# Gate computation moved to the next step, and head work moved between engines, in a fused retention and mixture-of-attention-heads kernel

## The chip, the cores and the metric

The kernel runs on one core of one Trainium2 chip. The metric is the device time of one execution, in microseconds (µs); the median of three executions is 523.59 µs (520.85 to 524.5).

The core has five engines that run side by side, each through its own list of instructions in order: TensorE (PE; its weight loads are shown as PEld), VectorE (DVE), ScalarE (ACT), GpSimd (POOL) and SyncE (SP, which issues the DMAs here). An instruction that has to wait holds up all that stand behind it on its engine.

## The reference

Two layers, in float32. The first is retention over 8 batches, 8 heads, 576 tokens and head size 64: `ret = 0.125 * (q k^T) * D`, with `D[i,j] = gamma_h^(i-j)` for `j <= i` and 0 above, and `x = ret v`. Heads side by side give `x` of shape (8, 576, 512). The second layer is a soft mixture of four causal attention heads ("experts") over `x`:

```
logits = x @ w_gate                      # (B, S, 4); the two largest are kept per token
w = softmax of the two kept              # divided by (sum + 1e-9)
q, k, v = x @ wq[e], x @ wk[e], x @ wv[e]
a = softmax(causal(0.125 * q k^T))       # divided by (sum + 1e-9)
out += mask_e * w_e * (a @ v @ wo[e])    # over the four experts
```

## The kernel before, in words

**Tiling.** Tokens of a batch are cut into chunks of 128, 128, 128, 128 and 64 (`CH`), which makes 40 chunks over the 8 batches. For the second layer they form two ranges: chunks 0 and 1 (256 tokens) and chunks 2 to 4 (320 tokens), `RNG`. Products that need more precision than one pass are made from a high and a low part (`xh`, `xl`, `wh`, `wl`): three passes of float32r matmuls.

**The loop.** The main loop (L494) runs steps n = 0 to 41, then `end()` follows. Step n computes the retention scores of chunk n (`qk`), finishes chunk n-1 (`result`: matmuls `old` and `own`, the product with the decay table `gi`, and the split into `xh` and `xl`), updates the running state from chunk n (`state`: matmuls `st`, sums `s`), starts the attention of tile n-6 (`scores`: matmuls `ss`, then softmax on DVE and ACT), transposes the probabilities of tile n-7 (`turn`: matmuls `pt` and copies to `pth`), does a share of projection work (`work`), normalizes tile n-6 (`normal`, DVE) and multiplies tile n-7 with the values (`values`: matmuls `ys`).

**Projection work.** `STEPS` sets it for each batch b: q and k of the first range in step 5b+3 and of the second in 5b+6 (`proj`, matmuls `pj`), values and gate logits of the first range in 5b+5 and of the second in 5b+7 (`vproj`, matmuls `pv`, results `vn` and `lg`), output projections in 5b+9 and 5b+12 (`outproj`, matmuls `po`). Batch 0 does its first parts piece by piece in steps 2 to 5, and the last batch some a step earlier.

**The gate.** `gate` (L260 to L284) makes the weights `wt` from the logits: ten small DVE groups (L268 to L284) with one exponential on ACT between them (L278), for which DVE waits. It is called by the last `vproj` of a range (L257). `normal` (L339) multiplies `wt` of its own tile's range into the reciprocal sums and scales the probabilities `p32` (L355). For tiles t = 0 and t = 2, the first of a range, that is one step after the `vproj` that ends the range.

**Order and buffers.** PE, DVE, ACT and POOL run in exactly the order in which the code issues to them (`manual_schedule`); the DMAs of SP are put in place by the framework. All PSUM tiles share one ring of eight banks (L49), so a matmul group also waits for the reader of the tile eight places before it.

**Head.** `decay(n+1)` (L92) in step n scales v of chunk n+1 by `gam` and, for chunks 1 to 4, makes that chunk's part of the table `gi` out of its first 128 columns; before the change both are POOL instructions, apart from chunk 0's v scaling on DVE. `result` multiplies by `gi` and makes `xl` on DVE for chunks 0 to 3 and on POOL from chunk 4 on (L182). Raw weights are fetched by `fetch` into two buffers (L198) and split by `weights` into high and low part (ACT L209, DVE L210): q and k in step 1, v in step 4, o in step 6.

## Time and profile before

| | |
|---|---|
| three executions | 523.59, 520.85, 524.5 µs |
| the profiled execution | 522.38 µs, its span 520.7 µs |
| PE busy, share of the span | 91% |
| DVE, ACT, POOL busy | 62%, 49%, 42% |
| mean TensorE clock granted, as a share of full speed | 0.961 |
| DMA traffic | 50.98 MB, mean 98 GB/s |

A row of the profile names engine, line and tiles as out<-in. In a timeline the first two numbers are the start in µs from the start of the span and the time from the first start to the last end of the instructions merged into the row (x4: four of them); a bracket at the end gives the idle time of the engine before the row and the instruction that ended it. In a table of waits the numbers are total µs, how often, and the longest. In a table of windows PEclk is the clock granted to TensorE in that stretch, 1.00 being full speed.

### The profile page before, as it was taken

The numbers are of one execution on the slowest core, as the hardware profiler recorded it, in microseconds if no ns is written. First come the engines' busy times: TensorE is split into PE (matmuls) and PEld (weight loads), VectorE is DVE, ScalarE is ACT, GpSimd is POOL, SyncE is SP. The second block draws the span as 40 slices with busy tenths as digits, with TensorE's granted clock in tenths as the row PEclk, the third lists the DMA queues.
The fourth block names the chain that finished last, engine by engine and source line by source line (L and its number), as shares of the span: only waits on it lengthen the run. The fifth ranks groups of instructions, "written<-read, shape, count | busy, mean of one in ns | idle before, by whom it ended". The sixth has DMA issues, their size and how long they took to land.

```text
span 520.7 us, 19016 instructions
## 1 busy us (share of the span) xinstructions
PE 472.8 (91%) x7996; PEld 413.5 (79%) x7996; DVE 323.4 (62%) x1136; ACT 256.8 (49%) x798; POOL 221.2 (42%) x279
## 2 busy tenths in 40 slices
PE   5768989999898989989899898989899898998996
PEld 3668968788788868889688797879788896877785
DVE  3655586754787556782767638775468737584463
ACT  2344546445464435645465354644447453654462
POOL 3834544543364434544246344554345443420201
PEclk9787989999899998999899998999989999999999
DMA  8943223404151241413223142431405101001022
GB/s 301 336 172 125 82 83 114 132 8 146 66 199 48 82 133 61 146 43 132 85 83 124 41 134 83 139 108 52 164 21 186 44 13 41 3 2 42 1 72 71
DMA packets 22516, 50.98 MB, mean 98 GB/s; under 512 B 2720, under 2 KB 11680, under 8 KB 22432
## 3 DMA queue, kind: packets, MB, share of 16 engines
q1 hardware_dynamic: 22432, 49.77, 27.8%
q8 instruction: 63, 1.03, 0.9%
q14 instruction: 21, 0.17, 0.1%
HBM read 40.33 MB, written 9.44 MB: 96 GB/s over the span
## 4 chain that ended last, share of the span: by engine, by line
PE 72%; DVE 17%; ACT 4%; issue 4%; DMA 2%; POOL 1%; SPq 0%; DVEq 0%; ACTq 0%; POOLq 0%
PE pj L224 22%; PE pv L248 11%; PE po L417 10%; PE pt L370 8%; PE ys L392 7%; PE ss L307 4%; PE ss L316 3%; PE qk L134 2%; DVE p L355 2%; DVE x L178 2%; DVE s L122 2%; DMA gi<-gi 2%; PE own L173 2%; PE st L114 1%; PE old L163 1%
## 5 line engine op out<-in xcount | busy, mean ns | idle before, releaser
L334 ACT ACTIVATE p<-p,nm 128x128 f32<-128x128 f32 (+4 forms) x144 | 83.0, 578 | 108.9 <-DVE nm L326 85.3
L355 DVE TENSOR_SCALAR p<-p,sm 128x128 f32<-128x128 f32 (+4 forms) x144 | 87.1, 663 | 1.4
L185 POOL TENSOR_TENSOR xl<-x,xh 128x512 fp32r<-128x512 f32 (+1 forms) x36 | 42.5, 1181 | 100.0 <-ACT xh L184 100.0
L370 PEld LDWEIGHTS pt<-con,p 128*128 128x128 f32 (+1 forms) x400 | 43.6, 143 | 49.1 <-issue 20.9
L370 PE MATMUL pt<-con,p 128*128 128x128 f32 (+1 forms) x400 | 58.3, 286 | 25.3 <-DVE x L178 12.9
L406 POOL CAST yh<-y 128x256 fp32r<-128x256 f32 (+1 forms) x39 | 15.9, 409 | 129.9 <-ACT y L405 129.9
L178 DVE TENSOR_TENSOR x<-x,own 128x256 f32<-128x256 f32 (+1 forms) x80 | 26.2, 360 | 65.2 <-ACT x L166 65.2
L326 DVE CUSTOM_DVE_ANT_0 p<-ss,mask 128x512 f32<-128x512 f32 (+3 forms) x128 | 56.2, 481 | 9.5 <-PE ss L307 7.9
L140 POOL TENSOR_SCALAR_AFFINE_SELECT p<-p 64x512 f32<-64x512 f32 (+1 forms) x80 | 49.6, 620 | 24.5 <-ACT p L137 21.7
L392 PE MATMUL ys<-pth,vn 128*64 128x128 f32 (+2 forms) x960 | 56.6, 262 | 0.0
L183 POOL TENSOR_TENSOR x<-x,gi 128x512 f32<-128x512 f32 (+1 forms) x36 | 41.7, 1159 | 27.9 <-DVE x L178 13.2
L392 PEld LDWEIGHTS ys<-pth,vn 128*64 128x64 f32 (+1 forms) x960 | 46.2, 136 | 8.1 <-issue 3.1
L253 DVE COPY lg<-pv 128x4 f32<-128x4 f32 (+1 forms) x40 | 6.4, 161 | 65.3 <-ACT vn L252 65.2
L307 PE MATMUL ss<-k,q 64*64 64x512 f32 (+3 forms) x512 | 43.8, 434 | 0.8 <-ACT p L137 0.5
L101 POOL TENSOR_TENSOR vk<-vk,con 128x512 f32<-128x512 f32 (+1 forms) x39 | 42.0, 1077 | 0.1
L373 DVE COPY pth<-pt 128x512 f32<-128x512 f32 (+3 forms) x80 | 37.7, 483 | 4.7 <-PE pt L370 4.3
L114 PE MATMUL st<-vk 64*64 64x64 f32 x1024 | 24.7, 224 | 10.0 <-POOL vk L101 5.5
L375 ACT ACTIVATE pth<-pt 128x512 f32<-128x512 f32 (+3 forms) x80 | 33.2, 420 | 0.5 <-PE pt L370 0.4
L248 PE MATMUL pv<-whv,xh 128*128 128x260 f32 (+1 forms) x160 | 27.1, 292 | 4.0 <-ACT whv L209 4.0
L224 PE MATMUL pj<-xh,whk 128*128 128x320 f32 (+1 forms) x128 | 27.9, 348 | 2.1 <-DVE s L122 1.3
L137 ACT ACTIVATE p<-qk 128x256 f32<-128x256 f32 (+1 forms) x80 | 24.6, 360 | 10.7 <-PE qk L134 10.6
L114 PEld LDWEIGHTS st<-vk 64*64 64x64 f32 x1024 | 20.4, 137 | 11.6 <-POOL vk L101 5.9
(89 smaller groups left out, 1034.2 us busy)
## 6 DMA issues: line engine op xcount, KB each, us to landing
x<-xf SPq DMA_DIRECT2D x32, 512.0 KB, 4.1
vk<-vkf SPq DMA_DIRECT2D x32, 512.0 KB, 5.4
out<-ot SPq DMA_DIRECT2D x32, 160.0 KB, 1.9
out<-ot SPq DMA_DIRECT2D x32, 128.0 KB, 1.8
raw<-wraw SPq DMA_DIRECT2D x4, 512.0 KB, 7.6
x<-xt SPq DMA_DIRECT2D x8, 256.0 KB, 2.8
vk<-vkt SPq DMA_DIRECT2D x8, 256.0 KB, 2.9
gi<-gi SPq DMA_DIRECT2D x1, 256.0 KB, 7.9
```

The costliest lines, as they stand in the source:

```text
L114: mm(ps[r][HALF[g], s, u], vk[HALF[r], s, 1, h], vk[HALF[r], s, 0, h], start=True, stop=True)
L140: gp.affine_select(w, w, pattern=[[0, 4 * k], [1, 64]], base=0, channel_multiplier=-1, compare_op=OP.is_ge, fill=0.0)
L185: e.tensor_sub(xl[:, :, l0:l0 + C], x32, f(xh[:, :, l0:l0 + C]))
L224: mm(ps, ww[:, kc, p * 128:(p + 1) * 128], xx[:, kc], start=(i == 0), stop=(i == 11))
L248: mm(ps[:C], xx[:, kc, l0:l0 + C], ww[:, kc], start=(i == 0), stop=(i == 11))
L307: mm(ps[2 * p + z][HALF[i]], q[p][HALF[z], l0 + 64 * i:l0 + 64 * i + 64], k[p][HALF[z], :w], start=True, stop=True)
L326: v.tensor_tensor_reduce(p32[:, e], ps[e], mask[:, 512 - w:], -1.0, BIG, OP.add, OP.min, nm[:, e:e + 1])
L334: act(p32[:, e], p32[:, e], AF.Exp, bias=bias, scale=-1.0, accum_out=sm[:, 0, e:e + 1])
L355: v.tensor_scalar(p32[:, e], p32[:, e], rs[:, e:e + 1], None, op0=OP.mult)
L370: nc.tensor.transpose(pt[rows, j - j0], p32[:, e, c0:c0 + jw], ident)
L392: mm(py[64 * z:64 * z + 64, p], VN[b, rr][0][jr, j - 2 * rr, e * D:(e + 1) * D], src, start=(j == 0), stop=(j == t))
L417: mm(ps, ww[:, p, d * 128:(d + 1) * 128], yy[:, p], start=(i == 0), stop=(i == 5))
```

## The change

1. `vproj` no longer calls `gate`; it notes the range in the list `GATES`. The new `gates()` computes what is noted there. The loop calls it in the next step, behind the softmax and the transposes' copies and ahead of `weights`, `work` and `normal`; `end()` calls it behind `values(LAST + 1)`.
2. In `decay` the parts of `gi` are made by four ACT instructions each (one for each of four column groups, with `fac` as scale) in place of one POOL instruction. The v scaling of chunks 1 to 3 moves from POOL to DVE.
3. In `result` the product with `gi` and the split of chunks 2 and 3 move from DVE to POOL.
4. `raw` has three buffers; the third weights (v) are fetched in step 1 and split in step 3, in place of steps 2 and 4.

```diff
@@ decay
         if 0 < n < 5:
-            gp.tensor_mul(gi[:, :, t0:t0 + C], gi[:, :, :C], fac[:, c].unsqueeze(2).to_broadcast([128, 4, C]))
-        (gp if n else v).tensor_mul(vv, vv, gam[...])
+            for kc in range(4):
+                act(gi[:, kc, t0:t0 + C], gi[:, kc, :C], AF.Copy, scale=fac[:, c, kc:kc + 1])
+        (gp if n > 3 else v).tensor_mul(vv, vv, gam[...])
@@ result
-        e = gp if n > 3 else v
+        e = gp if n > 1 else v
@@ fetch
-        RAW[n] = raw = ld.tile([128, kc, w], F32, name="raw", bufs=2)
+        RAW[n] = raw = ld.tile([128, kc, w], F32, name="raw", bufs=3)
@@ vproj
         if t == tiles[-1]:
-            gate(b, r)
+            GATES.append((b, r))
         yield
+    GATES = []
+    def gates():
+        while GATES:
+            gate(*GATES.pop())
@@ end
         values(LAST + 1)
+        gates()
         normal(LAST + 3)
@@ main loop
-        if n in (2, 4):
-            fetch("v" if n == 2 else "o")
+        if n in (1, 4):
+            fetch("v" if n == 1 else "o")
...
         run(turns)
-        for w in {1: "kq", 4: "v", 6: "o"}.get(n, ""):
+        gates()
+        for w in {1: "kq", 3: "v", 6: "o"}.get(n, ""):
             weights(w)
```

TensorE's list of instructions stays as it is, row for row. Three places where the other lists change follow. Line numbers of the changed file are higher by 1 in the first layer and by 8 from `gate` on.

DVE at the seam of steps 12 and 13 (batch 1's second range ends in step 12). Before, the end of the gate stands between the logits and the normalization (`sm`, `p`), which stands ahead of step 13's `x` and `s`:

```order
L277 TENSOR_TENSOR ex<-lg,mx 128x12
L279 SCALAR_TENSOR_TENSOR ex<-rk,ex 128x12
L280 TENSOR_REDUCE mx<-ex 128x3
L281 TENSOR_SCALAR mx<-mx 128x3
L282 RECIPROCAL mx<-mx 128x3
L284 TENSOR_TENSOR wt<-ex,mx 128x12
L346 TENSOR_SCALAR sm<-sm 128x4
L347 RECIPROCAL sm<-sm 128x4
L349 TENSOR_TENSOR sm<-sm,wt 128x4
L355 TENSOR_SCALAR p_2042<-p_2042,sm 128x256 x4
L178 TENSOR_TENSOR x_2225<-x_2225,own 128x2x128 x2
```

The same place in the changed kernel, from the copies of the logits on:

```order
L254 COPY lg<-pv 128x4 x2
L254 COPY lg<-pv 64x4
L256 COPY lg<-pv 64x4
L354 TENSOR_SCALAR sm<-sm 128x4
L355 RECIPROCAL sm<-sm 128x4
L357 TENSOR_TENSOR sm<-sm,wt 128x4
L363 TENSOR_SCALAR p_2054<-p_2054,sm 128x256 x4
L179 TENSOR_TENSOR x_2219<-x_2219,own 128x2x128 x2
L123 TENSOR_TENSOR s<-st,s 128x128 x4
```

Between the logits and the normalization the gate is gone; its rows (L276 to L292 there) follow behind step 13's softmax and last copy `pth`, ahead of step 13's own normalization.

ACT over step 13 in the changed kernel, from the values of step 12 (`vn`) to the first projection read out in step 13 (`k`); before the change the row `ex` stood between the two rows `vn 64x256` and `y`:

```order
L253 ACTIVATE vn_2122<-pv 128x256 x2
L253 ACTIVATE vn_2122<-pv 64x256
L413 ACTIVATE y_2184<-ys 128x256
L138 ACTIVATE p<-qk 128x256 x2
L167 ACTIVATE x_2219<-old 128x256 x2
L342 ACTIVATE p_2294,sm<-p_2294,nm 128x384 x2
L383 ACTIVATE pth<-pt 128x256
L342 ACTIVATE p_2294,sm<-p_2294,nm 128x384 x2
L383 ACTIVATE pth<-pt 128x256
L185 ACTIVATE xh_2215<-x_2219 128x4x128
L286 ACTIVATE ex<-ex 128x12
L230 ACTIVATE k_2344<-pj 128x256
```

The exponential of the gate now comes behind the step's softmax and its `xh`, and ahead of the projections' copies.

POOL in the head of the changed kernel, from step 0 to step 5; `AFFINE_SELECT` is the causal mask of `qk`:

```order
L141 AFFINE_SELECT p<-p 64x512 x8
L184 TENSOR_TENSOR x_438<-x_438,gi 128x512
L186 TENSOR_TENSOR xl_435<-x_438,xh_434 128x4x128
L102 TENSOR_TENSOR vk<-vk,con 128x256
L141 AFFINE_SELECT p<-p 64x256 x2
L184 TENSOR_TENSOR x_566<-x_566,gi 128x512
L186 TENSOR_TENSOR xl_435<-x_566,xh_434 128x4x128
L102 TENSOR_TENSOR vk<-vk,con 128x2x256
```

Before, each of the first three pairs of masks was followed by a `gi` and a `vk` row, and the rows `x` and `xl` of chunks 2 and 3 stood on DVE. The v scaling of chunk 5 (the last row) now stands behind the split of chunk 3.

## The prediction

> **What bounds the kernel now.** The page's busy times and its chain of work that ended last come first:

> ```profile
> PE 472.8 (91%) x7996; PEld 413.5 (79%) x7996; DVE 323.4 (62%) x1136; ACT 256.8 (49%) x798; POOL 221.2 (42%) x279
> PE 72%; DVE 17%; ACT 4%; issue 4%; DMA 2%; POOL 1%; SPq 0%; DVEq 0%; ACTq 0%; POOLq 0%
> ```

> TensorE carries the span, and the change leaves its list of work as it is. To be won are the 48 µs in which it is idle (520.7 less 472.8), and whatever it loses by running below full clock. DVE, with 17% of the chain, is what it mostly waits for. The table of TensorE's waits says where:

> ```profile
> PE pt L370 <- DVE x L178: 12.9, 8, 1.8
> PE pt L370 <- DVE p L355: 8.4, 7, 1.3
> PE st L114 <- ACT y L405: 1.7, 7, 0.5
> ```

> The transposes `pt` make up 21.3 of it, in 7 or 8 waits each: about one of each kind per batch. The timeline at the start of step 13, right behind the gate of step 12, shows the place of the longer kind:

> ```profile
> 127.18 0.21 DVE L268 TENSOR_TENSOR gd<-lg 128x48 f32<-128x48 f32 x1
> 128.35 0.21 ACT L278 ACTIVATE ex<-ex 128x12 f32<-128x12 f32 x1 [1.56 <-DVE ex L277]
> 129.44 1.51 PE L307 MATMUL ss<-k,q 64*64 64x384 f32 x15
> 130.06 0.16 DVE L346 TENSOR_SCALAR sm<-sm 128x4 f32<-128x4 f32 x1
> 132.30 0.74 DVE L178 TENSOR_TENSOR x<-x,own 128x256 f32<-128x256 f32 x2
> 132.77 0.77 PE L370 MATMUL pt<-con,p 128*128 128x128 f32 x4 [1.82 <-DVE x L178]
> 133.76 0.54 DVE L326 CUSTOM_DVE_ANT_0 p<-ss,mask 128x384 f32<-128x384 f32 x1
> 133.79 1.09 PE L370 MATMUL pt<-con,p 128*128 128x128 f32 x4 [0.25 <-DVE s L122]
> 137.09 0.63 PE L224 MATMUL pj<-xh,whq 128*128 128x256 f32 x4
> 138.52 0.64 PE L224 MATMUL pj<-xh,whk 128*128 128x256 f32 x4
> 141.46 1.09 PE L392 MATMUL ys<-pth,vn 128*64 128x128 f32 x16
> ```

> The gate holds DVE from 127.18 to 130.06. Only then come the normalization and the sums `x` and `s`, for whose banks the transposes wait 1.82 and 0.25 µs. Behind it lies a second loss, which the windows show:

> ```profile
> 73.00:75.00 2.00, 2.00 (x11) 2.00 (x10) 2.00 (x8) 1.99 (x7) 0.16 (x1) 0.50 0.03 8
> 134.00:136.00 2.00, 2.00 (x11) 2.00 (x11) 2.00 (x10) 1.66 (x6) 0.50 (x1) 0.50 0.04 8
> 441.00:443.00 2.00, 2.00 (x11) 2.00 (x11) 1.66 (x8) 2.00 (x8) 0.00 (x0) 0.50 0.00 0
> 137.00:141.00 4.00, 4.00 (x36) 4.00 (x35) 3.31 (x7) 1.95 (x7) 2.03 (x2) 1.00 0.00 0
> ```

> Behind the gap TensorE is full, but its granted clock is 0.50; from 137 on it is 1.00 again. The first and the last of the seven such seams are quoted; all seven have it. The gate of a first range costs less:

> ```profile
> 160.45 0.19 DVE L268 TENSOR_TENSOR gd<-lg 128x32 f32<-128x32 f32 x1
> 162.65 0.16 DVE L346 TENSOR_SCALAR sm<-sm 128x2 f32<-128x2 f32 x1
> 165.19 1.55 PE L370 MATMUL pt<-con,p 128*128 128x128 f32 x10 [1.12 <-DVE p L355]
> 167.00 0.82 PE L224 MATMUL pj<-xh,whk 128*128 128x320 f32 x4 [0.26 <-DVE s L122]
> 165.00:168.00 3.00, 2.47 (x17) 2.03 (x18) 3.00 (x19) 0.70 (x4) 1.28 (x1) 1.00 0.12 44
> ```

> There TensorE waits 1.12 and 0.26, and the clock stays at 1.00.

> **The change part by part.**

> *Gate of a second range* (seven seams). The normalization starts at 127.18 in place of 130.06. It takes 2.24 (130.06 to 132.30), so `x` runs from 129.42 to about 130.1 and `s` to 130.9; ACT no longer sits 1.56 µs idle at `ex`, so `x` has its input by then. TensorE ends `ss` at 130.95 (129.44 + 1.51), or some 0.3 earlier, as the wait of `st` for `y` (1.7 µs in 7 times, 0.24 each) goes too. So the waits of 1.82, 0.25 and 0.24 vanish: 2.31. What is late next: the first projection needs the bank that the softmax's first reduction frees, 0.54 behind `s`, at 131.4, when eight transposes from 130.6 on are done at 131.45. I charge 0.15 for it. For the clock: from 132.77 to 141.46 are 8.69, 0.25 of it wait. The price at full clock, and the cover for what follows below:

> ```profile
> 137.28 0.62 ACT L184 ACTIVATE xh<-x 128x512 fp32r<-128x512 f32 x1
> 144.19 0.75 DVE L178 TENSOR_TENSOR x<-x,own 128x256 f32<-128x256 f32 x2 [3.63 <-ACT x L166]
> 145.57 1.53 PE L370 MATMUL pt<-con,p 128*128 128x128 f32 x12
> 146.85 0.48 PE L417 MATMUL po<-yh,who 128*128 128x256 f32 x2
> 177.85 0.75 DVE L178 TENSOR_TENSOR x<-x,own 128x256 f32<-128x256 f32 x2 [4.90 <-ACT x L166]
> ```

> Twelve transposes take 1.28 from start to start (145.57 to 146.85), so eight take 0.85; twelve projections (137.09 to 138.52) take 1.43, so 48 take 5.72. The clock costs 8.69 - 0.25 - 6.57 = 1.87. The sum is 2.31 + 1.87 - 0.15 = 4.0 per seam, 28.0 for seven; the bounds are 2.16 (idle alone) and 4.18 (nothing new late).

> [...]

> *Gate of a first range* (six seams). DVE's 2.2 µs (160.45 to 162.65) go, and with them the waits of 1.12 and 0.26; the ten transposes and the second wait took 1.81 (165.19 to 167.00), and take 1.07 at the pace above. So 1.38 to 1.86 are saved. I take 1.7, nearer the upper end, because `s` is then done before `pt` ends: 10.2. The last batch's gate has a `pt` wait of this kind too (the seventh of the 8.4 µs): 1.0, with bounds 0.5 and 1.2.

> *Where the gate goes.* Its 2.9 or 2.2 µs land behind a softmax, in steps full of projections. Behind it on DVE stand that step's normalization and the next `x`, for which transposes and banks wait one step later. DVE idles 3.63 and 4.90 ahead of these `x`. The faster projections take 1.3 of the 3.63, so `x` would come 0.6 later at worst, and TensorE comes to it only 1.4 later (144.19 to 145.57). So it costs nothing; without that idle time all 2.9 would come back. On ACT the copies `k` and `q` stand behind `ex`, and their banks are needed again only eight tiles on.

> *Head.* These rows carry it:

> ```profile
> 11.24 1.04 POOL L100 TENSOR_TENSOR gi<-gi,con 128x512 f32<-128x512 f32 x1 [3.32 <-DMA gi<-gi]
> 36.18 1.24 PE L248 MATMUL pv<-whv,xh 128*128 128x260 f32 x4 [4.03 <-ACT whv L209]
> 41.21 0.69 PE L114 MATMUL st<-vk 64*64 64x64 f32 x32
> 45.92 0.69 PE L114 MATMUL st<-vk 64*64 64x64 f32 x32 [1.00 <-POOL vk L101]
> 47.11 0.94 PE L307 MATMUL ss<-k,q 64*64 64x128 f32 x16 [0.49 <-ACT p L137]
> 47.97 1.30 PE L224 MATMUL pj<-xh,whk 128*128 128x320 f32 x4
> L375 ACT ACTIVATE pth<-pt 128x128 f32<-128x128 f32 x16 | 4.0, 257 | 0.0
> L334 ACT ACTIVATE p<-p,nm 128x128 f32<-128x128 f32 x32 | 12.5, 393 | 25.9 <-DVE nm L326 25.9
> L183 POOL TENSOR_TENSOR x<-x,gi 128x512 f32<-128x512 f32 x28 | 35.9, 1281 | 24.6 <-PE pt L370 12.4 <-DVE x L178 10.5 <-POOL p L140 0.4
> L185 POOL TENSOR_TENSOR xl<-x,xh 128x512 fp32r<-128x512 f32 x28 | 36.6, 1307 | 83.7 <-ACT xh L184 83.7
> ```

> The trace has no ACT copy of 128 columns with a scale from memory; the nearest are a plain copy, 257 ns, and an exponential with a bias, 393. Four make 1.0 to 1.6; I take 1.1, by the copy. (1) The first four wait for the DMA of `gi` (11.2) ahead of ACT's copies of `x`, and the second four stand ahead of the q and k split; the v scaling on DVE gains back most of it. I put the first projections 0.5 later (0 to 1). (2) `whv` now stands ahead of chunk 3's copies, so `pv` can start near 33. But chunk 3's product and split now run on POOL (1.28 + 1.31) ahead of chunk 5's v scaling, whose `st` then starts near 39.7 in place of 41.21, behind a new gap of about 4 µs and so at half clock. Of the 4.03 I keep 0.6. (3) In step 6 the waits of 1.00 and 0.49 go with the gate's hold on ACT, 1.5; four projections took 1.30 there and 0.82 at 167.00, so with no gap ahead of them three such groups save 1.4. Sum: -0.5 + 0.6 + 1.5 + 1.4 = 3.0, bounds -1 and 6. The earlier fetch and third buffer of the v weights bring nothing by themselves: the split waited for ACT's order, not for a DMA.

> *Sum.* 28.0 + 10.2 + 1.0 + 3.0 = 42.2. The profiled execution took 522.4 (span 520.7), so 480.2. The median of the three runs is 1.2 above that execution and their lowest 1.5 below it, so I predict 480.

> **The rivals.**

> [...]

> *The gate's wait only moves.* If the normalization behind it ended after TensorE stands at the next `pt`, the 2.9 or 2.2 would come back as idle time there, the clock would fall there instead, and only the head's 3.0 would stay: 519. Against it stand the 3.63 and 4.90 µs in which DVE idles.

> *Slower: `ex` comes back late.* DVE stands in order behind ACT's `ex`, and ACT comes to it only after `xh`, which waits for POOL. Behind `ex` DVE needs 4.7 (128.35 to 132.30, and 0.74) until `x` is done, and TensorE needs it 9.8 behind the first projection (145.57 less 134.5, less 1.3). If `ex` starts later than 5 behind that projection, every further µs is idle time in 13 steps, plus 1.9 of clock; at 7.5 it would be 13 x (2.5 + 1.9) = 57 against the 42 gained: 537. Against it: `xh` is over at 137.9, 3.4 behind the first projection.

> **How the numbers follow.** Chances: the forecast 0.76, the slow clock stays 0.16, the wait moves 0.05, slower 0.03. The forecast's own best case is 522.4 - 7 x 4.18 - 6 x 1.86 - 1.2 - 6 = 475; a µs below it for the lowest of the runs makes the low end 474. The high end is the first rival's 498; the other two, 0.08, lie outside. A measurement of this kernel tells about 1% from no change. The first two cases are faster by more than that, 0.92; within 1% lies the moved wait, 0.05; slower is the last, 0.03.

> **What would show it.** Right: the waits of `pt` for `x` and `p` fall from 21.3 to under 4 µs, the windows with 0.50 behind the seams are gone and the mean clock rises from 0.961 to about 0.99; 48 projections behind a seam take 5.7; and in the head `st` of chunk 5 waits about 4 µs for POOL. Wrong: a `pt` wait for `p` one step later, windows of 0.50 that stay behind the seams, or DVE waiting at `ex` for more than 1 µs.

## The result, and the profile after

The changed kernel takes 484.34 µs (median of 4 runs, 482.29 to 485.27) against 523.34 (4 runs, 520.85 to 524.5) beside it: a ratio of 0.9255, 95% interval 0.9211 to 0.93. The forecast was 480, the range 474 to 498: faster, as forecast, by 4.3 less than forecast. The profiled execution took 484.3, its span 482.6, at a mean clock of 0.982.

The busy times and the chain that ended last, then the largest waits of TensorE (total µs, times, longest), after the change:

```profile
PE 458.3 (95%) x7996; PEld 401.6 (83%) x7996; DVE 314.0 (65%) x1135; ACT 260.0 (54%) x814; POOL 216.0 (45%) x276
PE 80%; DVE 9%; ACT 5%; issue 2%; DMA 2%; POOL 1%; SPq 0%; DVEq 0%; ACTq 0%; POOLq 0%
```

```profile
PE pt L378 <- DVE x L179: 3.5, 7, 0.6
PE old L164 <- DVE s L123: 2.9, 1, 2.9
PE st L115 <- POOL vk L102: 2.9, 1, 2.9
PE pj L225 <- ACT xh L185: 2.8, 1, 2.8
PE pt L378 <- DVE s L123: 1.7, 7, 0.2
```

DVE's share of the chain falls from 17% to 9%. The waits of `pt` for `p` are gone; those for `x` fall from 12.9 to 3.5. TensorE is idle for 24 µs (482.6 less 458.3) instead of 48, and its busy time falls by 14.5 with the same 7996 matmuls. By an estimate 9.3 of that is the slow clock behind the seven seams (1.33 each, worked out below); the rest was not split up. The windows behind two seams now show it at full clock:

```profile
182.50:184.50 2.00, 2.00 (x18) 2.00 (x18) 1.97 (x9) 2.00 (x8) 0.00 (x0) 1.00 0.06 18
238.50:240.50 2.00, 2.00 (x20) 2.00 (x19) 1.97 (x11) 2.00 (x8) 0.00 (x0) 1.00 0.19 78
```

No window behind any of the seven seams is below 1.00. One seam of the changed kernel in the timeline (the third of the seven; the one shown at 127 to 141 before was the second):

```profile
177.05 0.17 DVE L354 TENSOR_SCALAR sm<-sm 128x4 f32<-128x4 f32 x1
177.77 2.55 DVE L363 TENSOR_SCALAR p<-p,sm 128x256 f32<-128x256 f32 x4
177.80 0.73 POOL L415 TENSOR_TENSOR yl<-y,yh 128x256 fp32r<-128x256 f32 x1
178.49 1.43 POOL L141 TENSOR_SCALAR_AFFINE_SELECT p<-p 64x512 f32<-64x512 f32 x2
178.69 1.50 PE L315 MATMUL ss<-k,q 64*64 64x384 f32 x16
180.25 0.74 DVE L179 TENSOR_TENSOR x<-x,own 128x256 f32<-128x256 f32 x2
180.71 0.77 PE L378 MATMUL pt<-con,p 128*128 128x128 f32 x4 [0.52 <-DVE x L179]
181.73 0.63 PE L378 MATMUL pt<-con,p 128*128 128x128 f32 x4 [0.25 <-DVE s L123]
182.31 0.74 PE L225 MATMUL pj<-xh,whk 128*128 128x256 f32 x4
185.99 1.26 DVE L287 SCALAR_TENSOR_TENSOR ex<-rk,ex 128x12 f32<-128x12 f32 x1 [0.59 <-ACT ex L286]
188.19 1.09 PE L400 MATMUL ys<-pth,vn 128*64 128x128 f32 x16
```

The gate now runs behind the softmax, and DVE waits 0.59 for its exponential. But the normalization ahead of it takes 3.20 (177.05 to 180.25), not 2.24 as before: the scaling of `p` took 1.61 then (from 130.77) and takes 2.55 now. So TensorE still stops twice at the seam, 0.52 and 0.25, where I had charged 0.15 in all.

### The profile page after: what moved, and what is told of

Its sections match the earlier page's. It is cut to its first block, busy times and chain, and to the rows that moved or that the text cites. A ratio compares the mean times of both kernels' runs of the same rounds, so it can differ in the third digit from the quotient of the medians.

```text
span 482.6 us, 19026 instructions
## 1 busy us (share of the span) xinstructions
PE 458.3 (95%) x7996; PEld 401.6 (83%) x7996; DVE 314.0 (65%) x1135; ACT 260.0 (54%) x814; POOL 216.0 (45%) x276
## 4 chain that ended last, share of the span: by engine, by line
PE 80%; DVE 9%; ACT 5%; issue 2%; DMA 2%; POOL 1%; SPq 0%; DVEq 0%; ACTq 0%; POOLq 0%
PE pj L225 21%; PE pv L249 11%; PE ys L400 10%; PE po L425 10%; PE pt L378 9%; PE ss L315 5%; PE qk L135 4%; DVE p L363 3%; PE ss L324 3%; PE own L174 2%; PE st L115 2%; PE old L164 2%; DVE x L179 2%; DMA gi<-gi 2%; ACT p L138 1%
## 5 line engine op out<-in xcount | busy, mean ns | idle before, releaser
L186 POOL TENSOR_TENSOR xl<-x,xh 128x512 fp32r<-128x512 f32 (+1 forms) x38 | 44.6, 1174 | 97.3 <-ACT xh L185 97.3
L363 DVE TENSOR_SCALAR p<-p,sm 128x128 f32<-128x128 f32 (+4 forms) x144 | 70.7, 551 | 1.4
L414 POOL CAST yh<-y 128x256 fp32r<-128x256 f32 (+1 forms) x39 | 17.5, 449 | 112.2 <-ACT y L413 112.2
L378 PEld LDWEIGHTS pt<-con,p 128*128 128x128 f32 (+1 forms) x400 | 42.7, 139 | 28.7 <-issue 12.5
L334 DVE CUSTOM_DVE_ANT_0 p<-ss,mask 128x512 f32<-128x512 f32 (+3 forms) x128 | 56.2, 482 | 8.5 <-PE ss L315 8.5
L378 PE MATMUL pt<-con,p 128*128 128x128 f32 (+1 forms) x400 | 55.1, 280 | 7.0 <-DVE x L179 3.5
L184 POOL TENSOR_TENSOR x<-x,gi 128x512 f32<-128x512 f32 (+1 forms) x38 | 44.5, 1170 | 13.5 <-PE pt L378 8.7
L102 POOL TENSOR_TENSOR vk<-vk,con 128x512 f32<-128x512 f32 (+1 forms) x36 | 35.3, 980 | 0.0
L413 ACT ACTIVATE y<-ys 128x256 f32<-128x256 f32 (+1 forms) x39 | 14.1, 363 | 32.7 <-PE ys L400 32.3
L138 ACT ACTIVATE p<-qk 128x256 f32<-128x256 f32 (+1 forms) x80 | 24.6, 359 | 11.3 <-PE qk L135 11.3
L185 ACT ACTIVATE xh<-x 128x512 fp32r<-128x512 f32 (+1 forms) x40 | 23.2, 579 | 11.6 <-POOL x L184 8.0
L253 ACT ACTIVATE vn<-pv 128x256 f32<-128x256 f32 (+1 forms) x40 | 15.1, 381 | 26.5 <-PE pv L249 26.5
L425 PE MATMUL po<-yh,who 128*128 128x320 f32 (+1 forms) x128 | 28.8, 306 | 0.6 <-ACT yh L409 0.6
```

Of the source, the lines that this page charges most:

```text
L184: e.tensor_mul(x32, x32, gi[:, :, t0:t0 + C])
L186: e.tensor_sub(xl[:, :, l0:l0 + C], x32, f(xh[:, :, l0:l0 + C]))
L334: v.tensor_tensor_reduce(p32[:, e], ps[e], mask[:, 512 - w:], -1.0, BIG, OP.add, OP.min, nm[:, e:e + 1])
L363: v.tensor_scalar(p32[:, e], p32[:, e], rs[:, e:e + 1], None, op0=OP.mult)
L378: nc.tensor.transpose(pt[rows, j - j0], p32[:, e, c0:c0 + jw], ident)
L425: mm(ps, ww[:, p, d * 128:(d + 1) * 128], yy[:, p], start=(i == 0), stop=(i == 5))
```

## The experiments

All kernels compute the full result; three add work that it does not need, as their expectations say. Stage times come from the starts of rows in the timelines. A period is the time from one seam to the next, read at the first softmax row behind the seam.

### Which part carries the gain

*Gates alone*: the changed kernel with the head of the one before (`gi` on POOL, v scaling on POOL from chunk 1, `x` on DVE up to chunk 3, two raw buffers, v weights in steps 2 and 4).

> The gates in the next step as in the changed kernel, the head as before. Theory (the prediction's terms): the gates carry 28.0 + 10.2 + 1.0 and the head 3.0, so this run is some 3 us slower than the changed kernel, 487. In the changed kernel's trace kq1 begins only 0.26 us earlier, so most of the head's 3 us would have to be clock in the first 50 us. Rival: the head brings nothing, or takes something (first projection 0.92 later, ACT busy with gi): 484 or less.

Measured: 484.11 (ratio 0.9255, 0.9217 to 0.9293), equal to the whole change within its interval. The expectation's 487 does not come; the rival's "484 or less" does, within the noise.

*Head alone*: the changed kernel, with the gate back in `vproj`:

```diff
-            GATES.append((b, r))
+            gate(b, r)
```

> The head as in the changed kernel, the gates where they were. Theory: 523.3 less 3.0, so 520.4, with the wait of st of chunk 5 for POOL (2.9 us in the changed kernel) there again. Rival: 523 or more, since that wait eats what the earlier v projection brings. The seven 0.50 windows behind the seams stay under both.

Measured: 521.56 against 523.4 (ratio 0.9968, 0.9944 to 0.9991). A gain of 1.8 with an interval that just leaves out none, so neither 3.0 nor nothing.

*Only second ranges*: gates alone, with

```diff
-            GATES.append((b, r))
+            if r:
+                GATES.append((b, r))
+            else:
+                gate(b, r)
```

> The head as before; only the gates of second ranges moved, those of first ranges where they were. Theory: the terms 28.0 and 10.2 are separate, so this run is 10 us slower than the one with both gates moved: 497. Rival: the first ranges' gate stands beside work that is no bound (its clock stayed at 1.00), and moving it is worth half of that or less: 492 or less.

Measured: 500.82 (0.9577, 0.9527 to 0.9627), 16.7 slower than both gates moved, where 10 was expected: a first range's gate is worth more than its term, not less as the rival had it. The waits of TensorE split as the edit does, those for `x` as in the changed kernel and those for `p` as before it:

```profile
PE pt L380 <- DVE p L365: 8.2, 7, 1.3
PE pt L380 <- DVE x L178: 3.9, 8, 0.6
```

Its steady period is 57.89; before it is 61.27 (mean of six), with both gates moved 55.85. So a second range's gate is worth 3.38 per batch and a first range's 2.04. Six times 2.04 is 12.2 of the 16.7. The profiled executions differ by more, 20.2 in their spans: 4.8 of it ahead of the first seam, part of which is a later start of the first matmuls (`qk` at 6.10 instead of 5.07), and 1.6 in a stretch of half clock at 163 to 166 (such stretches come below).

### Is it the gap that makes the clock fall?

*Scores twice*: the kernel before, with TensorE's list made longer in front of the wait:

```diff
-            for p in range(2):
+            for p in list(range(2)) * (2 if t == 2 and m < LAST else 1):
```

> The kernel before, with the eight score matmuls of the tile of each of the seven seams issued twice into the same banks (same result, more work), which lengthens TensorE's list by about 1.5 us per seam exactly ahead of the wait for the normalization. Theory: the 0.50 windows come from TensorE's gap of 1.8 us; with the gap filled they vanish, the extra matmuls cost nothing, and 7 x 1.87 us are saved: 510. Rival 1: the clock falls for another reason (the kind of work behind the seam): 523, or up to 534 where the extra matmuls also cost their time. Rival 2: the gap is left at about a third and the clock falls for a shorter time: 515 to 520.

Measured: 514.58 (0.983, 0.9794 to 0.9867): faster by 1.7% with 112 matmuls more. The gate is where it was, and `x` comes no earlier; TensorE merely has work until 0.52 before it. The wait for `x` falls to the one of the changed kernel, and behind none of the seven seams is the clock low:

```profile
PE pt L370 <- DVE p L355: 8.5, 7, 1.3
PE pt L370 <- DVE x L178: 3.8, 8, 0.5
```

Its first four periods are 59.8 to 60.1 against 61.27, so some 1.4 is saved per seam, which is the clock alone. The 8.8 in all is less than the 13 of the expectation, because the clock costs less than the 1.87 that I gave it, and because it fell in this run behind two *first* ranges' gates, which had left it alone before:

```profile
283.21 1.55 PE L370 MATMUL pt<-con,p 128*128 128x128 f32 x10 [1.22 <-DVE p L355]
285.01 0.82 PE L224 MATMUL pj<-xh,whk 128*128 128x320 f32 x4 [0.26 <-DVE s L122]
343.01 1.55 PE L370 MATMUL pt<-con,p 128*128 128x128 f32 x10 [1.27 <-DVE p L355]
344.82 1.20 PE L224 MATMUL pj<-xh,whk 128*128 128x320 f32 x4 [0.25 <-DVE s L122]
```

```profile
280.22:283.63 3.41, 2.19 (x108) 1.97 (x101) 3.22 (x11) 1.00 (x4) 2.38 (x4) 1.00 0.49 150
283.63:287.05 3.42, 3.08 (x22) 2.62 (x21) 3.07 (x18) 1.74 (x8) 1.28 (x1) 1.00 0.03 8
341.65:345.06 3.41, 1.81 (x16) 1.27 (x13) 3.38 (x14) 0.00 (x0) 1.64 (x3) 1.00 0.44 142
345.06:348.48 3.42, 3.42 (x14) 3.42 (x14) 2.39 (x14) 3.11 (x12) 0.95 (x2) 0.50 0.00 0
```

Around the first gap TensorE is idle for 1.22 of one slot and 0.34 of the next, and the clock stays; around the second all 1.60 fall into one slot, and the next slot has half the clock.

*One or two sums more on DVE*: the changed kernel with the gap opened again (`range(2)` in the second kernel; `fl` is a tile that nothing else uses, zeroed on POOL at the start),

```diff
+        if n % 5 == 2 and 7 <= n <= 37:
+            for _ in range(1):
+                v.tensor_add(fl, fl, fl)
         for m in new:
             normal(m)
```

> The changed kernel with one DVE sum of an unused 128x512 tile (some 0.6 us, work that the result does not need) ahead of the normalization of each of the seven seams, which makes TensorE's gap there about 1.3 us where it is 0.77 now. Theory (the clock falls only behind a gap near 1.5 us and more; gaps of 1.3 at the first ranges' seams let it fall in about one of four): no or at most two 0.50 windows, 484.3 + 7 x 0.6 = 488.5, up to 492 with two windows. Rival (any lengthening of the gap costs the clock again): 484.3 + 7 x (0.6 + 1.87) = 501.6.

> The same with two such sums, which makes the gap about 1.9 us, as long as in the kernel before (2.07). Theory: 0.50 windows behind all seven seams, 484.3 + 7 x (1.2 + 1.87) = 505.8. [...]

Measured: 488.74 (0.9332, 0.9288 to 0.9376) and 497.7 (0.9499, 0.9437 to 0.9561). With one sum the gaps are 0.97 to 1.15 and no seam has a slow clock. The time is that of the first expectation, almost to the digit, but with some luck: the stop at a seam grew by 0.47 instead of 0.6, and in the profiled run the clock fell once in the last batch, behind a wait of 1.17. With two the gaps are 1.44 to 1.80 and five of seven seams have it, so the truth lies between the theory and the 492.7 that the two sums would give by their own time alone (484.3 + 7 x 1.2). The windows behind two seams of that run, the first behind a wait of 1.57, the second behind 1.44:

```profile
186.00:188.00 2.00, 2.00 (x11) 2.00 (x11) 1.97 (x10) 2.00 (x8) 0.00 (x0) 0.50 0.03 10
243.50:245.50 2.00, 2.00 (x16) 1.81 (x17) 2.00 (x8) 1.50 (x6) 0.64 (x1) 1.00 0.10 41
```

Over the profiles of all fourteen kernels, every wait of `pt` from 0.9 µs up (behind the first 50 µs), by length, and how often the clock fell to 0.50 behind it:

| wait of `pt`, µs | cases | clock fell |
|---|---|---|
| 0.93 to 1.01 | 11 | 0 |
| 1.08 to 1.27 | 38 | 6 |
| 1.44 to 1.58 | 6 | 5 |
| 1.80 to 1.82 | 15 | 14 |

The length of a wait does not settle it by itself: between 1.08 and 1.27 the clock falls sometimes. TensorE's idle time in one slot of the grid, as the profile shows it, comes close to settling it. Over the same fourteen profiles, all slots behind the first 50 µs that ran at full clock:

| TensorE idle in the slot, µs | slots | clock 0.50 in the next slot |
|---|---|---|
| below 1.40 | 1714 | 0 |
| 1.40 to 1.54 | 9 | 3 |
| above 1.54 | 23 | 22 |

The kernels' ends are not in the table: before, a slot idle for 1.87 (515.78 to 519.19) has a slot at full clock behind it, in which the kernel ends (520.7). The one exception above 1.54 is the first seam of the run with two sums, idle for 1.80 of a slot. This bound, of about 1.5 µs in a slot of 3.41, is read off the traces afterwards; no run was made to test it. It says why the table of waits looks as it does. A seam with a wait of 0.97 to 1.01 and the 0.25 behind it cannot bring a slot to 1.40; with one of 1.80 to 1.82, 1.80 or more came together in one slot in all 15 cases; in between the place in the grid decides. The seven seams of one kernel are not seven separate trials, either: before, their period of 61.27 is nearly 18 slots (61.44), so their place in the grid shifts little from one to the next.

### What is left at the seam

*Normalization first*: the changed kernel, with DVE's normalization of the seam's tile issued ahead of the step's projections instead of behind them.

```diff
+        early = n % 5 == 2 and 7 <= n <= 37
+        if early:
+            for m in new:
+                normal(m)
         run(work(n))
-        for m in new:
-            normal(m)
+        if not early:
+            for m in new:
+                normal(m)
```

> The changed kernel with the normalization of each of the seven seams ahead of the step's projections in DVE's list, so it is not behind the last logits. Theory: the 0.52 + 0.25 us that TensorE still waits at a seam go, 7 x 0.77 = 5.4: 479. Rival: the sums x and s, not the normalization, hold DVE there, and the wait stays at half or more: 482 or more.

Measured: 474.87 (0.9072, 0.9025 to 0.9118): 9.5 less than the changed kernel where 5.4 was expected. The seam has no wait left:

```profile
168.85 2.97 DVE L363 TENSOR_SCALAR p<-p,sm 128x256 f32<-128x256 f32 x4
168.97 1.39 POOL L186 TENSOR_TENSOR xl<-x,xh 128x512 fp32r<-128x512 f32 x1 [2.72 <-ACT xh L185]
170.31 1.09 POOL L102 TENSOR_TENSOR vk<-vk,con 128x512 f32<-128x512 f32 x1
...
176.08 1.48 PE L315 MATMUL ss<-k,q 64*64 64x384 f32 x15
176.15 0.75 DVE L179 TENSOR_TENSOR x<-x,own 128x256 f32<-128x256 f32 x2 [1.78 <-ACT x L167]
177.49 1.09 PE L378 MATMUL pt<-con,p 128*128 128x128 f32 x8
178.34 0.71 PE L225 MATMUL pj<-xh,whk 128*128 128x256 f32 x4
```

The scaling of `p` ends 5.7 µs ahead of its use (still slow, now beside POOL's `xl` and `vk`), `x` is done before the scores are, and the eight transposes run in one piece. A stop costs more than the wait that is shown for it. This one table shows the seam in all its states (second seams in the middle of the run, µs between starts):

| kernel | `ss` to `pt` | `pt` to `pj` | 48 `pj` to `ys` |
|---|---|---|---|
| before | 3.47 | 1.60 to 1.76 | 6.88 to 7.45 |
| changed | 2.02 | 1.60 | 5.89 |
| two sums, clock fallen | 3.08 | 1.60 to 1.74 | 7.13 to 7.45 |
| normalization first | 1.44 | 0.85 | 5.86 |

From the changed kernel to this one a seam loses 0.58 + 0.75 + 0.03 = 1.36, of which 0.77 is shown as wait. That is the 9.5 µs: 7 x 1.36. Most of what is not shown as wait stands between `pt` and `pj`, where 0.75 goes and only 0.25 of it was a wait; why such a stop costs that much more was not worked out.

### The head

*v of chunks 4 and 5 on DVE*: the changed kernel, with `gp if n > 5 else v` in `decay`.

> The changed kernel with the v scaling of chunks 4 and 5 on DVE too, so that st of chunk 5 does not wait for POOL's list. Theory: that wait of 2.88 us and the half clock behind it (3.2 us at 0.50 and more) are gone: 484.3 less 2.9 to 4.5, so 480. Rival: DVE is late in its own list there and st waits as long for it, or the projections' end is the bound: 483 to 485.

Measured: 483.38 (0.9233, 0.9189 to 0.9277): not told apart from 484.34. It lies in the range of the rival. The first seam comes 1.9 earlier, but two other waits of `st` stand in place of the 2.88: 1.58 for `vk` on POOL and 1.19 for `lg` on DVE. In the profiled run the clock also fell once in the last batch, behind a `pt` wait of 1.15, which costs 1.54 there (8.75 from `pj` to `ys`, 7.21 with the normalization first). What the move is worth without that fall stays open.

*Old head under the normalization first*, and *`gi` back on POOL* under it:

> The normalization first at the seven seams, gates moved, and the head as before the change. Theory, from the two runs so far (gates alone 484.11, changed kernel 484.34): next to the moved gates the change of the head is worth nothing, so this run equals the one with the changed head: 474.9, within 1. Rival (the prediction's term for the head): 3.0 slower, 477.9.

> Normalization first on the changed kernel, with the decay table back on POOL (one operation of about 1.0 to 1.4 us in place of four copies on ACT of 1.28 us together). Theory: pj waits 2.9 us for xh because ACT is behind with the four copies; with them gone the first projection is 1 us earlier, and st of chunk 5 waits longer for POOL: between 474 and 475. Rival: ACT was the bound of the whole head, and 2 us or more are won: 473 or less.

Measured: 476.23 (0.9123, 0.9096 to 0.9151) and 475.61 (0.9093, 0.9063 to 0.9123). Against 474.87 (0.9072, 0.9025 to 0.9118) the intervals overlap: by the medians the changed head is worth 1.4 here, a little over the 1 that the expectation allowed and not told from nothing. Which engine makes `gi` makes no difference that can be seen: 475.61 is a little above the theory's 474 to 475 and well above the rival's 473.

*v first on POOL*: normalization first, `gi` on POOL but behind the v scaling, v of chunks 5 and 6 on DVE, `x` on DVE up to chunk 3, the v weights early as in the changed kernel.

```diff
+        (gp if n not in (0, 5, 6) else v).tensor_mul(vv, vv, gam[...])
         if 0 < n < 5:
-            for kc in range(4):
-                act(gi[:, kc, t0:t0 + C], gi[:, kc, :C], AF.Copy, scale=fac[:, c, kc:kc + 1])
-        (gp if n > 3 else v).tensor_mul(vv, vv, gam[...])
+            gp.tensor_mul(gi[:, :, t0:t0 + C], gi[:, :, :C], fac[:, c].unsqueeze(2).to_broadcast([128, 4, C]))
@@ result
-        e = gp if n > 1 else v
+        e = gp if n > 3 else v
```

> Normalization first and gates moved; in the head POOL scales v of chunks 1 to 4 ahead of its decay table instead of behind it, DVE scales v of chunks 5 and 6, the decay table stays on POOL, x of steps up to 3 on DVE as before, and the third weights come early as in the changed kernel. Theory: the three waits of the changed head (old for s 3.0, pj for xh 2.9, st for POOL 2.9, all beside the half clock) shrink to about half: 474.9 less 4, 471. Rival: TensorE's start is bound by what arrives (x, v and the first weights), and a wait that goes comes back at the next operation: 474 to 475.

Then the same with the v weights late again (two raw buffers, fetched in step 2, split in step 4):

> The run with v first on POOL (469.15), but the third weights fetched in step 2 into two buffers and split in step 4, as in the kernel before. Theory: pv waits 4 us for whv again, with some 4 us of half clock behind it: 469.2 plus 4 to 6, so 473 to 475. Rival (the wait is only taken over from the next operations, as with the changed head, where pv starts 2.1 us earlier and kq1 0.26): 470 or less.

Measured: 469.15 (0.8978, 0.8954 to 0.9002), the best version, 15 µs below the changed kernel and 1.9 better than its expectation; and 474.44 (0.9074, 0.9039 to 0.9109) with the weights late, as that run's theory had it. The heads of the changed kernel, of v first, and of v first with late weights:

```profile
10.77 1.28 ACT L101 ACTIVATE gi<-gi,con 128x128 f32<-128x128 f32 x4 [3.29 <-DMA gi<-gi]
21.95 0.73 PE L225 MATMUL pj<-xh,whk 128*128 128x256 f32 x4 [2.83 <-ACT xh L185]
34.07 0.74 PE L249 MATMUL pv<-whv,xh 128*128 128x260 f32 x4 [0.74 <-ACT k L230]
38.15 1.26 POOL L186 TENSOR_TENSOR xl<-x,xh 128x512 fp32r<-128x512 f32 x1 [0.74 <-ACT xh L185]
39.38 1.04 POOL L102 TENSOR_TENSOR vk<-vk,con 128x512 f32<-128x512 f32 x1
40.47 1.14 PE L115 MATMUL st<-vk 64*64 64x64 f32 x32 [2.88 <-POOL vk L102]
47.71 0.85 PE L225 MATMUL pj<-xh,whk 128*128 128x320 f32 x4
```

```profile
32.72 0.74 PE L248 MATMUL pv<-whv,xh 128*128 128x260 f32 x4
37.36 0.69 PE L114 MATMUL st<-vk 64*64 64x64 f32 x32 [1.32 <-issue]
41.94 0.85 PE L224 MATMUL pj<-xh,whk 128*128 128x320 f32 x4
```

```profile
38.01 1.23 PE L248 MATMUL pv<-whv,xh 128*128 128x260 f32 x4 [3.64 <-ACT whv L209]
43.30 0.86 PE L114 MATMUL st<-vk 64*64 64x64 f32 x32
47.97 0.85 PE L224 MATMUL pj<-xh,whk 128*128 128x320 f32 x4
```

With the weights early and the v scaling first in POOL's list, the projections of step 6 begin at 41.94 instead of 47.71; with the weights late they are back at 47.97. The early weights are worth 5.3 µs here, and in the changed kernel they are given back at `st`, 6.4 behind `pv`, by the v scaling that stands behind `xl` on POOL. By these rows that is where the head's gain went. Part of it is clock: it is 0.50 from 39.97 to 46.80 in the changed kernel and from 36.95 to 43.78 with the weights late, and 1.00 over both stretches in the best version. The expectation's theory, three waits cut to half, is met by one of them only: those of `old` and of the first `pj` are still 2.5 and 2.0 (2.9 and 2.8 in the changed kernel), that of `st` is 1.3 in place of 2.9. How much of the 5.7 below the run with normalization first comes from the order on POOL and how much from DVE's share was not tried apart.

## Why the prediction was right, and where it was off

**The bound.** Right. TensorE waited for DVE because the gate stood ahead of the normalization; with the gates alone moved all of the change's gain is there.

**The slow clock behind the gaps.** Right as a mechanism: the clock no longer falls when the gap is filled with other work (scores twice: behind none of the seven seams), and falls again when the gap is opened by work that has nothing to do with the gate (two sums: behind five of seven). The case in which the slow clock stays (0.16) is refuted by both. No run shows its 498, the upper end of the range, nor the 23.9 for idle time alone that lead to it; in its place the gates alone came to 484.11, and in the changed kernel no window behind a seam is below 1.00. The size was too high: 1.87 per seam, measured 1.2 to 1.6, on average 1.33 (transposes and projections together take 8.64 to 9.05 before and 7.49 after, from start to start). The step that failed is the price of eight transposes, 0.85, taken from twelve that run in one piece. Eight that stop for a bank in between take 1.60 at full clock too, and of that difference of 0.75 all but the 0.25 of wait was put down to the clock. Where the stop goes, with the normalization first, the 0.85 comes out. The gap as the cause was right; that the gap's place in the grid of 3.41 µs takes part in it was not seen.

**The new wait, 0.15.** This is the term that failed most. "It takes 2.24 (130.06 to 132.30)" was carried over to the new place; there it takes 3.20, as the scaling of `p` now runs beside two POOL operations instead of the end of one (the last section has the evidence). What is left at the seam is 0.52 + 0.25 of wait and, by the run with the normalization first, 1.36 in all. So a second range's gate gave 3.38 in place of 4.0, below the forecast but above the lower bound of 2.16.

**First ranges.** 1.7 was forecast, 2.04 is measured, a little over the upper bound of 1.86. All of its wait goes (no row of `pt` waiting for `p` is left), and it was 1.25 to 1.27 in most batches where I had priced the one with 1.12.

**Where the gate goes: free.** Right. No wait appeared one step later, and DVE waits 0.59 at `ex`. The rivals of the moved wait and of the late `ex` have nothing for them.

**Head, 3.0.** The sum came out wrong. With the gates in place it is worth 1.8, with the gates moved nothing that can be told from none (0.2 slower in one pair, 1.4 faster in the other). Of its 2.9 for step 6, 1.9 belonged to the gates: with the gates alone the wait of 0.49 is gone, and with it the slow clock (four projections take 0.85 there). The wait of 1.00 was not the gate's doing: with the gates alone it is still 0.94. The first projection came 0.9 later, at 21.95 against 21.03 (0.5 forecast, up to 1); `pv` came at 34.07 (33 forecast), and `st` of chunk 5 at 40.47 behind 2.88 of wait (39.7 and about 4 forecast). The sentence that the earlier fetch brings nothing by itself was not contradicted in this head, but as a statement on the weights it is: fetched and split early they are worth 5.3 once POOL does not stand in the way.

**The sum.** Priced were 39.2 for the gates and 3.0 for the head; 39.3 and about nothing came, by the medians. The 39.2 was hit by errors that cancel: with the gates alone a batch gains 5.4 instead of 5.7, but the first seam comes 4.9 earlier in the profile and the stretch from the last one to the end is 3.1 shorter, 8.0 together where one seam and the last batch were priced at 5.0. The 1.9 of step 6 belong there.

**What was to be seen.** The 0.50 windows behind the seams are gone, the mean clock is 0.982 (about 0.99 forecast) and 48 projections take 5.89 (5.7). The waits of `pt` for `x` and `p` are 3.5, all of it for `x`: under the 4 that was named, though well over the 1.05 that seven times 0.15 would make. Those for `s`, which the sign left out, add 1.7.

## What to carry to other kernels

Price the next wait with the durations of its new neighbours: an operation that is moved up runs beside other engines' work and may take half as long again there (the normalization: 3.20 in place of 2.24). A stop of TensorE cost its idle time, some more that the waits do not show (1.36 in all at a seam, 0.77 of it wait), and here 3.41 µs of half clock once more than 1.54 µs of idle time had come together in one slot of the clock's grid (22 of 23 slots); filling the gap removed the last of these, even with useless work (scores twice: 8.8 less in all). And when an early start in the head brings nothing, look at the next operation that the freed engine must wait for, and change the order there.

## What the runs showed of the hardware

The scaling of four 128x256 tiles on DVE took 1.61 before, beside the end of a POOL mask, 2.55 after, beside two POOL operations, and 2.97 with the normalization first, beside two others. In the changed kernel's seam the four take between 333 and 912 ns each (minimum, median, maximum):

```profile
L363 DVE TENSOR_SCALAR p<-p,sm x4: 333/772/912, 177.8 to 180.0; 128x256 f32<-128x256 f32 x4
```

Over the whole kernel it is the shape that stands beside POOL's work which is slow. Of 32 scalings of 128x256, 7 overlapped a POOL instruction before and 21 after; of 32 of 128x128, 14 and 5. Before and after the change, in the groups by shape (total µs, mean ns):

```profile
L355 DVE TENSOR_SCALAR p<-p,sm 128x256 f32<-128x256 f32 x32 | 12.4, 447 | 0.3
L355 DVE TENSOR_SCALAR p<-p,sm 128x128 f32<-128x128 f32 x32 | 18.0, 624 | 0.3
```

```profile
L363 DVE TENSOR_SCALAR p<-p,sm 128x256 f32<-128x256 f32 x32 | 18.9, 650 | 0.3
L363 DVE TENSOR_SCALAR p<-p,sm 128x128 f32<-128x128 f32 x32 | 7.1, 286 | 0.3
```

A tile of half the size took longer before, and less than half as long after. No run took POOL's work away by itself, but the traces point one way: over all fourteen profiles the 212 scalings of a 128x256 tile that ran while POOL did nothing took 332 to 356 ns each, and the 236 others took 352 to 1395. In the seam above the three of 742 to 912 ns each end 148 to 149 ns behind a POOL instruction (`yl` of 732 ns, masks of 712 and 657), and the fourth, begun after the last mask, takes 333. By what means POOL's work holds DVE's up is not shown.

The moved gate meets the same thing. Its small operation `ex<-rk,ex` (128x8 or 128x12) took 166 to 173 ns in all 66 cases without POOL beside it. In the changed kernel 14 of its 16 cases take 1.25 to 1.27 µs and end 20 to 27 ns behind the POOL instruction that was running; the row at 185.99 in the seam above is one. It costs nothing there, since no wait hangs on it.
